# Batch 1's v by casting transfers on the software queue, and w_in one chunk of v later, in a fused attention and feed-forward kernel

## The chip, the core and the metric

The kernel runs on one core of a Trainium2 chip. The metric is the device time of one execution in microseconds (us), the median over runs. The names are those of the profile: PE (TensorE, with PEld for its weight loads), DVE (VectorE), ACT (ScalarE), POOL (GpSimd) and SP (SyncE, which here only issues transfers). POOL issues the transfers of the software queue (q0), SP those of the hardware queue (q1).

## What is computed

For 8 batches of 8 heads, 576 tokens and 64 features, two attentions are added: a local one, in which a token sees its neighbours at a distance under 4, and one over means of 4 tokens, whose result is repeated 4 times. The sum, laid out as 4608 tokens by 512 features, goes through two matrix products with a gate between them.

```python
q_d = q.reshape(B, H, Sd, factor, D).mean(axis=3)      # k_d and v_d likewise, factor 4
out_up = np.repeat(sm_attn(q_d, k_d, v_d), factor, axis=2)
mask = np.abs(pos[:, None] - pos[None, :]) < factor
out_local = np.matmul(softmax(where(mask, scores, -1e9)), v)
x = (out_up + out_local).transpose(0, 2, 1, 3).reshape(B * S, H * D)
h = x @ w_in                                            # 512 -> 2048
out = (h * sigmoid(1.702 * h)) @ w_out                  # 2048 -> 512
```

All inputs are float32 in the memory outside the core; the matrix work is in bf16.

## The kernel before

**Groups and batches.** The feed-forward part runs over `n_groups` = 9 groups of 512 tokens. Group g needs the attention of batches up to g, so the loop over g computes group g and lays batch g + 1's attention (`attention`) between its matmuls, at places counted in sixteenths (`POS_0` for g = 0, `POS` later). Batch 0's attention stands by itself ahead of the loop, and its last part is mixed with the first matmuls of group 0 (`part`, `turned`). `mm1` multiplies by w_in and ACT applies the gate (`silu`); `mm2` multiplies by w_out. In group 0, `mm2` takes w_out by quarters (`load_w_out(0)` to `load_w_out(3)`): its order of 64 matmuls needs the third quarter from matmul 32 on, and the fourth from 48.

**The order is written out.** Every engine runs its instructions in the order of the source; there is no scheduler. A dependency holds a whole engine's queue. In the built program each software-queue transfer also waits until the eighth one before it has landed, and SP's transfers do the same among themselves.

**How v comes in.** `load_v` issues ten transfers on SP, five chunks i of two halves `par`, 64 partitions by 8 heads by 64 features each, float32 into the tile `vf`. `prep_v` then casts a chunk into the bf16 tile `vbs[b % 2]` (65 columns a head: the last holds ones). For batch 0 the casts are spread: chunks 0 and 1 on ACT, 2 to 4 on DVE. For batch 1 POOL does five casts. `load_v4` fetches v in a second layout for the means; batches 0 and 1 form those means on PE instead (`prep_vd_pe`, from all five chunks of `vbs`, line 312; the result is copied out by ACT in line 321). For batch 1 that stands at `VDP_0` = 52, which is matmul 36 of `mm2`.

**Gates.** To hold a transfer back, a one-element copy writes into its target and reads what it is to wait for. Line 728 (POOL) holds `load_w_in(0, 512)` until a part of v 0's second chunk is there. `load_v(1)` is held by a DVE copy (line 708) until the first quarter of w_out has landed. Line 808 (POOL) holds `load_w_out(2)` until v 1's fourth chunk is there.

**q and k.** `load_qk` brings both by casting transfers on the software queue. `prep_qk` transposes them on DVE (line 260), and `pool_qk` adds groups of four on POOL (lines 276 and 285: four instructions for a batch's half of the heads). `scores` (line 351) and `scores_d` (line 369) are the two products on PE; ACT takes the exponentials (`exp_local`, `exp_down`). `av_local` (line 408) and `av_down` (line 430) multiply by v; `normalise` is DVE (lines 441 and 443). For batch 0, `transp_sum` (lines 483, 493, 507) turns and adds both results on PE, and `copy_x` (lines 520 and 524) copies them on ACT to `xT`.

Of the kernel before, what the change touches and what calls it, by code (L numbers as in the profile page):

```python
# [10 lines left out]
AF = mybir.ActivationFunctionType  # L11
# [8 lines left out]
def kernel(  # L20
# [9 lines left out]
    nc = tc.nc  # L30
# [41 lines left out]
    def ps_tile(n=None):  # L72
        if n is None:
            n = turn["a"] % 3
            turn["a"] += 1
        return PA[n]
# [130 lines left out]
    def load_v(b, gate=None):  # L207
# [4 lines left out]
        for i in range(5):  # L212
            for par in range(2):
# [6 lines left out]
                    ),  # L220
                )

    def load_v4(b):
        for kc in range(3):
            for j in range(2):
                nc.sync.dma_start(
                    out=v4[64 * j : 64 * j + 48, kc],
                    in_=bass.AP(
                        tensor=v.tensor,
                        offset=v[b, j].offset + kc * 48 * 4 * D,  # L230
                        ap=[[4 * D, 48], [2 * S * D, HP], [1, 4 * D]],
                    ),
                )
# [32 lines left out]
    def prep_qk(b, qd):  # L266
        prep_1("k", b, qd)
        prep_1("q", b, qd)

    def pool_qk(b, qd, names="kq"):  # L270
        for name, src in (("k", kT), ("q", qT)):
            if name not in names:
                continue
            sv = src[b, qd].rearrange("p (j f) a -> p j f a", f=4)
            t1 = work.tile([128, SD, 2, 2], FP32, name="pq", tag="pq")
            nc.gpsimd.tensor_tensor(  # L276
                out=t1, in0=sv[:, :, 0:2, :], in1=sv[:, :, 2:4, :], op=ALU.add
            )
            if name == "k":
                dst = kdT[qd][:, 0:SD, :]  # L280
            else:
                t = work.tile([128, SD, 2], BF16, name=f"qdT{qd}", tag=f"qdT{qd}", bufs=1)
                qdT[b, qd] = t
                dst = t
            nc.gpsimd.tensor_tensor(
                out=dst, in0=t1[:, :, 0, :], in1=t1[:, :, 1, :], op=ALU.add
            )
# [73 lines left out]

    def scores_d(b, qd, sd=None):
        sd = sd or ps_tile()
        for kc in range(3):
            for a in range(2):
                for r in range(4):
                    rows = slice(32 * r, 32 * r + 32)
                    j = r % 2
                    nc.tensor.matmul(  # L369
                        sd[64 * j : 64 * j + 64, r // 2, SD * kc : SD * kc + SD],  # L370
                        lhsT=kdT[qd][rows, 48 * kc : 48 * kc + 64, a],
                        rhs=qdT[b, qd][rows, :, a],
                        start=(a == 0), stop=(a == 1),
                        tile_position=(32 * r, 64 * j),
                    )
        return sd
# [8 lines left out]
    def exp_down(qd, sd):  # L385
        nc.scalar.activation(  # L386
            out=eds[qd][:, :, 0:432], in_=sd[:, :, 0:432],
            func=AF.Exp, scale=inv_sqrt_d / 16.0,
        )
# [12 lines left out]
    def av_local(b, hp, o):  # L402
        E, vb = es[hp], vbs[b % 2]
        for i in range(5):
            for par in range(2):
                for j in range(2):
                    pos = j if par == 0 else 1 - j
                    nc.tensor.matmul(  # L408
                        o[64 * pos : 64 * pos + 64, par, 65 * i : 65 * i + 65],
                        lhsT=E[64 * par : 64 * par + 64, j, 60 * i : 60 * i + 64],  # L410
                        rhs=vb[64 * par : 64 * par + 64, i, 2 * hp + j, :],
                        start=True, stop=True,
                        tile_position=(64 * par, 64 * pos),
                    )

    def av_down(b, hp, o):
        Ed, vd, u = eds[hp // 2], vds[b % 2], hp % 2

        blocks = [(kc, x, 0) for kc in range(3) for x in range(2)]
        blocks += [(0, 0, 1), (0, 1, 1), (1, 0, 1), (2, 0, 1)]  # L420
        if True:
            for kc, x, c2 in blocks:
                for j in range(2):
                    pos = j if x == 0 else 1 - j
                    c0 = 65 * (5 + c2)
                    q0 = SD * kc + 48 * (min(x + c2, 1) + x)
                    last = x == c2 == 1
                    if last:
                        q0 = 0
                    nc.tensor.matmul(  # L430
                        o[64 * pos : 64 * pos + 64, j, c0 : c0 + 65],
                        lhsT=Ed[64 * j : 64 * j + 48, u, q0 : q0 + 64],
                        rhs=vd[64 * j : 64 * j + 48, kc, hp, :],
                        start=(kc == 0), stop=(kc == 2 or last),
                        tile_position=(64 * j, 64 * pos),
                    )

    def normalise(o):
        ov = o[:, :, 0:455].rearrange("p x (c e) -> p x c e", e=65)
        rc = work.tile([128, 2, 7, 1], FP32, name="rc", tag="rc")  # L440
        nc.vector.reciprocal(rc, ov[:, :, :, 64:65])  # L441
        y = work.tile([128, 2, 7, D], BF16, name="y", tag="y", bufs=4)
        nc.vector.tensor_tensor(  # L443
            out=y, in0=ov[:, :, :, 0:D],
            in1=rc.to_broadcast([128, 2, 7, D]), op=ALU.mult,
        )
        return y
# [69 lines left out]
    def copy_x(b, hp, x):  # L517
        t0 = b * S
        for par in range(2):
            nc.scalar.copy(  # L520
                out=sub(xT[hp], t0 + 3 + 57 * par, (114, 5), (1, 57)),
                in_=sub(x[par], 3 - 3 * par, (57, 5), (1, 57)),
            )
            nc.scalar.copy(
                out=sub(xT[hp], t0 + 573 * par, (1, 3)),
                in_=sub(x[par], 285 * par, (1, 3)),
            )
# [40 lines left out]
    def warm(n):  # L568
        if n:
            t = pm_tile()  # L570
            for _ in range(n):
                nc.tensor.matmul(
                    t, lhsT=wz[:, 0:128], rhs=wz, start=True, stop=True
                )
# [132 lines left out]
    def after(src, eng):  # L707
        return lambda t: eng.tensor_copy(out=t, in_=src)
# [16 lines left out]
    sp = scores(0, 0, barred=True)  # L725
    exp_local(0, sp)
    prep_qk(0, 1)
    nc.gpsimd.tensor_copy(out=w_in_bf[0:1, 0, 0:1], in_=vf[0][0:1, 1, 0, 0:1])
    load_w_in(0, 512)
    pool_qk(0, 1)  # L730
    load_w_in(512, 512)
    load_w_in(1024, 1024)
    for qd in range(NQ):
# [16 lines left out]
        prep_v(0, nc.vector, i=slice(i, i + 1))  # L750
    warm(6)
    prep_vd_pe(0, PA[2])
    o[0] = PA[0]
    av_local(0, 0, o[0])
    av_down(0, 0, o[0])
    y[0] = normalise(o[0])
    sd = scores_d(0, 1, PA[1])
    exp_down(1, sd)
    nc.scalar.preload_act_table_set("silu_and_others")
    for hp in range(1, 3):  # L760
        o[hp] = PA[hp]
        av_local(0, hp, o[hp])
        av_down(0, hp, o[hp])
        y[hp] = normalise(o[hp])
    warm(1)

    gT0 = new_gT()
    acc = PM + [PA[n][:, u, :] for n in (1, 2, 0) for u in range(2)]
# [25 lines left out]
        silu(gT0, ffc, acc[ffc])  # L794

    def loads_2():
        load_v(2)
        load_v4(2)

    for g in range(n_groups):  # L800
        b = g + 1
        if g == 0:
            prep_qk(1, 0)
            pool_qk(1, 0)
            prep_qk(1, 1)
            load_v(1, gate=after(w_out_bf[0:1, 0, 0:1], nc.vector))
            pool_qk(1, 1)
            nc.gpsimd.tensor_copy(
                out=w_out_bf[0:1, 8, 0:1], in_=vf[1][0:1, 3, 0, 0:1]
            )  # L810
            load_w_out(2)
            load_w_out(3)
            for i in range(5):
                prep_v(1, nc.gpsimd, i=slice(i, i + 1))
            for qd in range(NQ):
                load_qk(2, qd)
            loads_2()
        elif b < B:
            if b > 2:
                load_v4(b)  # L820
            prep_qk(b, 0)
            pool_qk(b, 0)
            if b + 1 < B:
                for qd in range(NQ):
                    load_qk(b + 1, qd)
            prep_v(b, nc.gpsimd)
            if b + 1 < B:
                load_v(b + 1)
            prep_qk(b, 1)
            pool_qk(b, 1)  # L830
            prep_v4(b, nc.gpsimd)
        steps = {}
        if b < B:
            for n, f in zip(POS if g else POS_0, attention(b, None if g else (1, 2))):
                steps.setdefault(n, []).append(f)
            if g == 0:
                steps.setdefault(VDP_0, []).append(lambda: prep_vd_pe(1, PA[2]))
        gT = new_gT() if g else gT0
        mm1(g, gT, steps, 0 if g else 6)
        mm2(g, gT, {n - 16: f for n, f in steps.items() if n >= 16})  # L840
# [30 lines left out]
```

The softmax here doesn't subtract the row's maximum and nothing guards it: scores larger than these inputs give would overflow.

## Time and profile before

| what | value |
|---|---|
| median of 8 runs | 334.02 us (333.24 to 335.21) |
| the profiled execution's own time | 334.83 us |
| its span, first to last instruction | 333.0 us |
| PE busy | 318.4 us (96%), 5043 matmuls |
| ACT busy | 184.5 us (55%) |
| POOL busy | 138.2 us (42%) |
| DVE busy | 130.8 us (39%) |
| hardware queue q1 | 55056 packets, 26.95 MB, 35.3% of 16 engines' span |
| software queue q0 | 8304 packets, 13.63 MB, 23.7% |

The span is the time between the first and the last instruction of one profiled execution; that execution took 1.8 us more than its span. Busy time is summed over the whole span, so a high share says which engine is used most, not what a stretch waits for. A transfer's bytes are counted as they arrive: a cast from float32 to bf16 reads twice what is shown.

### The profile page before, as it was taken

The page shows a single profiled execution, that of the slowest core. Times are in us where ns is not written, and L with a number is a line of the kernel's source. Part 1 is how long each engine was busy: PE and PEld are TensorE (multiplying, and loading weights), DVE is VectorE, ACT ScalarE, POOL GpSimd, SP SyncE. Part 2 cuts the span into 40 slices and gives each one's busy share as a digit, 9 for nine tenths or more (in the row PEclk, how much of TensorE's full clock was granted, in tenths as well). Part 3 has the DMA queues.
Part 4 walks back from the last instruction along what each step waited for, and adds up shares of the span by engine and source line. Part 5 has one row for each costly group of instructions (what it writes and reads, how often), then busy time and mean ns, then how long its engine had stood idle before and what let it go on. Part 6 is the DMA issues. An engine that isn't in the chain of part 4 may idle for free.

```text
span 333.0 us, 11272 instructions
## 1 busy us (share of the span) xinstructions
PE 318.4 (96%) x5043; PEld 160.2 (48%) x5043; DVE 130.8 (39%) x213; ACT 184.5 (55%) x323; POOL 138.2 (42%) x168
## 2 busy tenths in 40 slices
PE   8758999999999999999999999999999999999995
PEld 3445445444554455445544454445544554444444
DVE  4837302582277216730773067406750570000000
ACT  2542487266745774566656664666466746425711
POOL 7791752019901990099109910992089000000000
PEclk9955899999999999999999999999999999999999
DMA  7999989997922993199519941993180110011011
GB/s 127 181 180 210 178 151 198 191 221 155 192 76 73 205 197 101 39 216 178 144 37 213 201 121 42 205 205 101 66 174 3 35 65 31 2 64 63 2 58 68
DMA packets 63552, 41.36 MB, mean 124 GB/s; under 512 B 44048, under 2 KB 54416, under 8 KB 63504
## 3 DMA queue, kind: packets, MB, share of 16 engines
q1 hardware_dynamic: 55056, 26.95, 35.3%
q0 software_dynamic: 8304, 13.63, 23.7%
q8 instruction: 39, 0.64, 0.8%
q14 instruction: 9, 0.07, 0.1%
q10 hardware_dynamic: 144, 0.07, 0.1%
HBM read 44.83 MB, written 9.44 MB: 163 GB/s over the span
## 4 chain that ended last, share of the span: by engine, by line
PE 89%; SPq 3%; DVE 2%; DMA 2%; issue 1%; ACT 1%; DVEq 0%; ACTq 0%
PE pm L616 36%; PE pm L672 35%; SPq L214 3%; PE pa L351 3%; PE pa L616 2%; PE pa L430 2%; PE pa L408 2%; PE pa L369 2%; DMA vf<-in_v_dram 2%; PE pa L457 2%; PE pa L672 1%; PE pm L687 1%; DVE y L443 1%; PE pa L483 1%; ACT vd L321 0%
## 5 line engine op out<-in xcount | busy, mean ns | idle before, releaser
L616 PE MATMUL pm<-xT,w_in_bf 128*128 128x512 bf16 x544 | 122.0, 381 | 0.5 <-DVE xT L559 0.5
L672 PE MATMUL pm<-w_out_bf,gT 128*128 128x512 bf16 x528 | 121.7, 380 | 0.0
L627 ACT ACTIVATE gT<-pm 128x512 bf16<-128x512 f32 x136 | 81.0, 598 | 44.5 <-PE pm L616 44.5
L616 PEld LDWEIGHTS <-w_in_bf 128*128 128x128 bf16 x576 | 55.8, 98 | 68.0 <-issue 2.0
L672 PEld LDWEIGHTS <-gT 128*128 128x128 bf16 x560 | 51.8, 98 | 59.5 <-issue 0.2
L276 POOL TENSOR_TENSOR pq<-kT 128x576 f32<-128x576 bf16 x16 | 18.5, 1159 | 106.9 <-DVE kT L260 106.9
L394 DVE TENSOR_TENSOR es<-es,mask 128x600 bf16<-128x600 bf16 x28 | 20.0, 729 | 97.1 <-ACT es L380 96.3
L657 ACT ACTIVATE osb<-pm 128x512 f32<-128x512 f32 (+2 forms) x35 | 20.8, 594 | 40.0 <-PE pm L672 36.1
L532 ACT COPY od<-pa 128x384 f32<-128x384 f32 (+1 forms) x56 | 18.4, 412 | 31.0 <-DVE y L443 18.7
L443 DVE TENSOR_TENSOR y<-pa,rc 128x896 bf16<-128x896 f32 x32 | 34.9, 1092 | 1.1
L553 DVE TENSOR_TENSOR xT<-pa,od 128x570 bf16<-128x570 f32 x28 | 21.1, 753 | 10.6 <-ACT od L532 10.5
L380 ACT ACTIVATE es<-pa 128x600 bf16<-128x600 f32 x32 | 19.8, 668 | 7.3 <-PE pa L351 7.0
L297 POOL TENSOR_TENSOR v<-v 112x512 f32<-112x512 f32 x18 | 22.8, 1265 | 0.0
L659 DVE TENSOR_SCALAR osb<-pm 128x128 f32<-128x128 f32 x1 | 0.3, 291 | 55.3 <-ACT osb L657 55.3
L260 DVE STREAM_TRANSPOSE kT<-kb 128x576 f32<-128x576 f32 x16 | 20.0, 1251 | 3.1 <-DMA kb<-in_k_dram 3.0
L260 DVE STREAM_TRANSPOSE qT<-qb 128x576 f32<-128x576 f32 x16 | 19.9, 1243 | 1.3 <-DMA qb<-in_q_dram 1.0
L276 POOL TENSOR_TENSOR pq<-qT 128x576 f32<-128x576 bf16 x16 | 18.5, 1156 | 0.0
L291 POOL CAST vb<-vf 128x2560 bf16<-128x2560 f32 (+1 forms) x11 | 17.0, 1572 | 0.0
L441 DVE RECIPROCAL rc<-pa 128x14 f32<-128x14 f32 x32 | 7.7, 241 | 23.6 <-PE pa L430 23.6
L351 PE MATMUL pa<-qT,kT 32*64 32x60 bf16 x1280 | 13.8, 203 | 2.1 <-issue 1.9
L386 ACT ACTIVATE ed<-pa 128x864 bf16<-128x864 f32 x16 | 14.3, 897 | 1.5 <-PE pa L369 1.5
L351 PEld LDWEIGHTS <-kT 32*64 32x64 bf16 x1280 | 11.9, 104 | 6.8 <-issue 5.6
(86 smaller groups left out, 254.9 us busy)
## 6 DMA issues: line engine op xcount, KB each, us to landing
vf<-in_v_dram SPq DMA_DIRECT2D x80, 128.0 KB, 5.3
out_dram<-osb SPq DMA_DIRECT2D x35, 256.0 KB, 2.0
v<-in_v_dram SPq DMA_DIRECT2D x36, 192.0 KB, 5.2
kb<-in_k_dram POOLq DMA_DIRECT2D x16, 288.0 KB, 6.7
qb<-in_q_dram POOLq DMA_DIRECT2D x16, 288.0 KB, 7.6
w_out_bf<-in_moe_w_out_dram POOLq DMA_DIRECT2D x4, 512.0 KB, 12.7
w_in_bf<-in_moe_w_in_dram POOLq DMA_DIRECT2D x2, 512.0 KB, 6.0
w_in_bf<-in_moe_w_in_dram POOLq DMA_DIRECT2D x1, 1024.0 KB, 9.9
```

The costliest lines, as they stand in the source:

```text
L260: nc.vector.transpose(out=t32.rearrange("p (i c) -> p c i", c=18), in_=store[b, qd].bitcast(FP32).rearrange("p (c d) -> p c d", c=18),)
L276: nc.gpsimd.tensor_tensor(out=t1, in0=sv[:, :, 0:2, :], in1=sv[:, :, 2:4, :], op=ALU.add)
L297: eng.tensor_tensor(out=t1[0:112], in0=x[:, :, 0:2, :], in1=x[:, :, 2:4, :], op=ALU.add)
L351: nc.tensor.matmul(sp[r // 2][64 * par : 64 * par + 64, r % 2, 60 * i : 60 * i + 60], lhsT=kT[b, qd][rows, k0 : k0 + 64, a], rhs=qT[b, qd] ...
L380: nc.scalar.activation(out=es[2 * qd + u][:, :, 0:300], in_=sp[u][:, :, 0:300], func=AF.Exp, scale=inv_sqrt_d,)
L394: nc.vector.tensor_tensor(out=ev, in0=ev, in1=mask, op=ALU.mult)
L443: nc.vector.tensor_tensor(out=y, in0=ov[:, :, :, 0:D], in1=rc.to_broadcast([128, 2, 7, D]), op=ALU.mult,)
L553: eng.tensor_tensor(out=sub(xT[hp], t0 + 3, (57, 2), (114, 5), (1, 57)), in0=sub(x, 3, (509, 2), (57, 5), (1, 57)), in1=sub(od, 3, (57, 2) ...
L616: nc.tensor.matmul(acc, lhsT=w_in_bf[:, dmc, ffc * 128 : (ffc + 1) * 128], rhs=xT[dmc][:, g * TG : g * TG + TG], start=(dmc == 0), stop=(d ...
L627: nc.scalar.activation(out=gT[:, ffc, :], in_=acc, func=AF.Silu, scale=GELU_SCALE)
L657: eng.activation(out=osb, in_=ap, func=AF.Copy, scale=1.0 / GELU_SCALE)
L672: nc.tensor.matmul(ops[t], lhsT=gT[:, ffc, t * 128 : (t + 1) * 128], rhs=w_out_bf[:, ffc, :], start=(ffc == 0), stop=(ffc == n_ffc - 1),)
```

## The change

1. The gate of `load_w_in(0, 512)` reads v 0's chunk 2 instead of chunk 1, and the k half of `pool_qk(0, 1)` moves ahead of it on POOL.
2. In batch 0's attention, the local products of heads 0 and 1 come first, then the two `av_down`; `scores_d(0, 1)` writes to the two banks `PM` instead of `PA[1]`, and its exponential becomes two instructions of 432 columns. One `warm` matmul then stands ahead of `av(0, 2, 2)`.
3. `copy_x` of the last pair of heads does its second half (`par` = 1) on DVE.
4. v 1 is no longer loaded by SP and cast by POOL. `load_vb` issues ten casting transfers on the software queue, straight into `vbs[1]`; they stand on POOL around the two `pool_qk(1, ...)`, two ahead of the first, four behind it and four behind the second, and the third and fourth quarter of w_out are issued after them. Both gates of that stage go. Both `prep_qk(1, ...)` stand ahead of them.
5. `loads_2` (v 2 and its second layout, on SP) moves from ahead of the group to place 42 of group 0, that is matmul 26 of `mm2`, and is gated on v 1's fourth chunk.

```diff
+    def load_vb(b, i):
+        for par in range(2):
+            nc.gpsimd.dma_start(
+                out=vbs[b % 2][64 * par : 64 * par + 64, i, :, 0:D],
+                in_=bass.AP(
+                    tensor=v.tensor,
+                    offset=v[b, 0].offset + (114 * i + KSTART[par]) * D,
+                    ap=[[D, 64], [S * D, H], [1, D]],
+                ),
+            )
...
     def scores_d(b, qd, sd=None):
         sd = sd or ps_tile()
+        bank = sd if sd is PM else [sd[:, u, :] for u in range(2)]
...
-                        sd[64 * j : 64 * j + 64, r // 2, SD * kc : SD * kc + SD],
+                        bank[r // 2][64 * j : 64 * j + 64, SD * kc : SD * kc + SD],
...
         for par in range(2):
-            nc.scalar.copy(
+            cp = nc.vector.tensor_copy if par and hp == HP - 1 else nc.scalar.copy
+            cp(
...
     prep_qk(0, 1)
-    nc.gpsimd.tensor_copy(out=w_in_bf[0:1, 0, 0:1], in_=vf[0][0:1, 1, 0, 0:1])
+    pool_qk(0, 1, "k")
+    nc.gpsimd.tensor_copy(out=w_in_bf[0:1, 0, 0:1], in_=vf[0][0:1, 2, 0, 0:1])
     load_w_in(0, 512)
-    pool_qk(0, 1)
+    pool_qk(0, 1, "q")
...
     prep_vd_pe(0, PA[2])
-    o[0] = PA[0]
-    av_local(0, 0, o[0])
-    av_down(0, 0, o[0])
-    y[0] = normalise(o[0])
-    sd = scores_d(0, 1, PA[1])
-    exp_down(1, sd)
-    nc.scalar.preload_act_table_set("silu_and_others")
-    for hp in range(1, 3):
+    for hp in range(2):
         o[hp] = PA[hp]
         av_local(0, hp, o[hp])
+    for hp in range(2):
         av_down(0, hp, o[hp])
         y[hp] = normalise(o[hp])
+    scores_d(0, 1, PM)
+    for u in range(2):
+        nc.scalar.activation(
+            out=eds[1][:, u, 0:432], in_=PM[u][:, 0:432],
+            func=AF.Exp, scale=inv_sqrt_d / 16.0,
+        )
+    nc.scalar.preload_act_table_set("silu_and_others")
     warm(1)
+    o[2] = av(0, 2, 2)
+    y[2] = normalise(o[2])
...
     def loads_2():
-        load_v(2)
+        load_v(2, gate=after(vbs[1][0:1, 3, 0, 0:1], nc.vector))
         load_v4(2)
...
             prep_qk(1, 0)
+            prep_qk(1, 1)
+            load_vb(1, 0)
             pool_qk(1, 0)
-            prep_qk(1, 1)
-            load_v(1, gate=after(w_out_bf[0:1, 0, 0:1], nc.vector))
+            load_vb(1, 1)
+            load_vb(1, 2)
             pool_qk(1, 1)
-            nc.gpsimd.tensor_copy(
-                out=w_out_bf[0:1, 8, 0:1], in_=vf[1][0:1, 3, 0, 0:1]
-            )
+            load_vb(1, 3)
+            load_vb(1, 4)
             load_w_out(2)
             load_w_out(3)
-            for i in range(5):
-                prep_v(1, nc.gpsimd, i=slice(i, i + 1))
             for qd in range(NQ):
                 load_qk(2, qd)
-            loads_2()
...
             if g == 0:
+                steps.setdefault(42, []).append(loads_2)
                 steps.setdefault(VDP_0, []).append(lambda: prep_vd_pe(1, PA[2]))
```

## The prediction

> **What bounds the kernel now.** First the page's slices of the span (8.3 us each): PE is full from the seventh slice on, so a change can win or lose only in the opening, or by opening a gap later.
>
> ```profile
> PE   8758999999999999999999999999999999999995
> PEclk9955899999999999999999999999999999999999
> DMA  7999989997922993199519941993180110011011
> ```
>
> PE has gaps in the first four slices, its clock is halved in slices 3 and 4, and the DMA engines are full there. Next the chain of waits, 13 to 37 us:
>
> ```profile
> 13.63 6.47 DMA vf<-in_v_dram
> 20.19 0.44 DVE vb L291
> 20.67 0.44 PE pa L312 x2
> 21.13 0.81 ACT vd L321
> ...
> 23.43 0.90 ACT ed L386
> 24.38 0.49 PE pa L408 x18
> ...
> 26.34 0.48 PE pm L483 x2
> ...
> 29.34 1.35 issue
> 30.69 0.42 PE pa L507 x12
> 31.11 0.96 PE pm L616 x2
> ...
> 36.71 0.28 PE pa L507 x20
> ```
>
> The opening waits for the last transfer of v 0 (chunk 4): issued at 13.63, landed at 20.10. The queues between 14.2 and 18.2 us say why:
>
> ```profile
> q0 software_dynamic: 515, 0.51, 89.5%
> q1 hardware_dynamic: 560, 0.14, 20.6%
> ```
>
> All 512 packets of the first w_in piece pass here, while v's queue has 20.6% of the engines. From 40.5 to 46 us, alone, v's 256-byte packets pass at 4229 in 5.5 us, 770 per us. Chunk 4 is 1024 packets; alone it would need 1.3 us. After this chain PE is busy without a gap of 0.15 us from 36.36 to 49.11 (the table by stage has 12.75 of 12.75 us).
>
> **The change, part by part.**
>
> *The gate.* POOL's timeline has the gate at 12.13 and the w_in issue at 12.60; its data begin about 14.2. Chunk 2's first half landed at 13.41, so the gate passes near 13.5 and the issue comes near 14.0, data near 15.6. In the 1.4 us gained chunk 4's 1024 packets pass at 700 to 800 per us, nearly all; they land near 16.5 (17.8 if a quarter is left behind w_in). Then DVE is next: in its timeline the casts of chunks 2 and 3 end at 18.06. Chunk 4's cast (0.43) ends at 18.5, against 20.63: **2.1 us** earlier. The k half of `pool_qk` fits into POOL's wait of 1.26 us ahead of the gate; the q half then ends near 17, earlier than the 17.78 of before. Behind it on POOL stand the other w_in pieces, so they come no later; w_in's first piece lands near 19 as before and is wanted at 28.5 at the earliest.
>
> *The order of batch 0's attention.* From PE's chunk 4 matmuls (20.67) to `transp_sum` (26.27) it is 5.6 us, with PE gaps of 0.47 (for vd) and 0.99 (for ed) in its timeline. With heads 0 and 1 together the first gap is covered by the second `av_local` (0.49). The product into `PM` ends about 3.2 us after chunk 4's matmuls; the two exponentials (0.5 each, from 0.9 for 864 columns) hold `warm` and `av_down` of pair 2 for 0.5 to 0.6. I get 5.25 us: **0.35 us** gained. `normalise` runs beside it and is ready 2 us before its reader.
>
> *`copy_x` on DVE.* ACT's four copies end at 37.87 and the matmuls that need them start at 40.39, so the path gains nothing. But batch 1's four transposes now queue on DVE behind a copy that waits for PE's last `transp_sum` (ends 36.99), where they began at 30.84. Nobody near needs them: `scores(1, 0)` is at 49.11. POOL does: see below.
>
> *v 1.* Taken away: five POOL casts (2.83 us), two gates, ten SP transfers. Added: ten POOL issues. Issues of 512 packets (w_in, w_out) took 0.75 to 0.81 us, of 128 packets (k, q) 0.56; `load_vb` has 512, so 0.78 each[...]. The data, which the trace does not show in this form: 256 bytes read, 128 written a packet. Nearest rows: plain 256-byte packets, 86.3% of 16 engines for 4229 in 5.5 us, 18 ns; casts with 1024 bytes written (20.2 to 22 us: 347 packets, 119.7%) 99 ns and 2048 bytes (23.5 to 26.8: 336, 111.0%) 174 ns. The straight line through the two casts gives 33 ns at 128 bytes. That is 32 packets an engine x 33 = 1.06 us, over the 1.15 at which cast packets overlap: 0.9 us a transfer (0.5 from the plain row). I take 0.9. [...] But this trace's four k and q transfers of 288 KB, issued 0.55 apart, landed at 30.7, 32.2, 33.6, 34.9: 1.4 us each[...]. [...]
>
> Now the chain on POOL, counted from the end of `transp_sum(3)` (T = 36.99 before): DVE's copy 0.5, first transpose 1.26, `pool_qk(1, 0)` 3.7 (32.25 to 35.94 in its timeline), four issues 3.1, `pool_qk(1, 1)` 3.7, four issues 3.1: the third quarter of w_out is issued at T + 15.4.
>
> ```profile
> DMA to landing us min/median/max: 5.9/7.5/9.2
> ```
>
> This answer for the two later quarters gives the third 5.9 us from issue to landing, of which, by its packets, 1.7 led to the first data and 2.9 was data. With v's last data ending near T + 17.5 and 2.9 + 1.0 behind them: T + 21.4. PE wants that quarter at 58.53 = T + 21.5. **Before, it landed at 51.83, T + 14.8; the change spends those 6.7 us of slack to the last 0.1.** v 1 itself is complete near T + 18.5 and wanted at T + 22.5 (59.48); the fourth quarter lands near T + 24.3, wanted at T + 28.8 (65.75); the pooled k and q are ready at T + 5.5 and T + 12.3, wanted at T + 12.8 and T + 16.5. I put **0.2 us** for the third quarter's expected lateness. The first two issues wait for w_in's last piece (28.45 before), with only `pool_qk(1, 0)` behind them, which waits longer for DVE. The four k and q issues of batch 2 move from 50.24 to about T + 17 and land by T + 30 = 67; DVE wants them at 72.33.
>
> *`loads_2` later.* Its DVE gate sits behind the masks (55.4) and finds chunk 3 there. v 2 would be complete about 69 (68.72 before) and POOL casts it at 79.48; the second layout lands by 77 (75.56), used at 85.50. SP's four stores behind it come 1 to 2 us later, and ACT has four buffers with the next store at 91.5. Nothing on the path.
>
> *The clock.* From 15.88 to 36.36 the table by stage grants PE half its clock, then all of it. The last 10.24 us of that in thirds:
>
> ```profile
> 26.12:29.53 3.41, 3.21 (x91) 2.52 (x91) 3.02 (x5) 0.83 (x4) 0.00 (x0) 0.50 1.11 211
> 29.53:32.95 3.42, 2.26 (x32) 1.18 (x35) 2.04 (x3) 0.83 (x4) 0.70 (x1) 0.50 1.11 209
> 32.95:36.36 3.41, 3.41 (x32) 1.34 (x34) 3.09 (x3) 0.83 (x4) 3.25 (x5) 0.50 1.22 205
> ```
>
> In columns: window, length, PE, PEld, DVE, ACT, POOL busy, granted clock, DMA. [...] the third stretch is the first with PE full. Of wide matmuls (line 616) the three hold 0, 1.03 and 2.74 us. If the end stood at 36.36 whatever PE does, as the row alone says, 2.45 us gained at half clock would be worth 1.2. [...] I take 2.45.
>
> **Sum.** 2.1 + 0.35 = 2.45, less 0.2: 2.25 us. On the profiled execution's own 334.83: 332.6. That execution is 0.8 above the median of 334.02, so the forecast is **331.8 us**. A measurement of this kernel can tell about 0.3%, 1.0 us.
>
> **The rivals.**
>
> *Half of it.* The half clock ends where it did: 334.02 - 1.2 = 332.8, lateness left out. For it: the trace's 36.36 is one event[...]. [...]
>
> *The gain is used up.* Either chunk 4's packets still straggle behind w_in (a quarter of them to 18 costs nothing, half of them to 19.2 costs 1.2), or the third quarter is 1.5 to 2 late: 334.02 - 2.45 + 1.75 = 333.3.
>
> *Slower: the third quarter of w_out comes late on the software queue.* It decides from 2.5 us lateness. Through the data: v's last four transfers start at T + 13.95, so break-even lies at 1.55 us a transfer, 55 to 58 ns a packet; from 1.8 us on, it is clearly slower. At 1.9 us even the middle four (data from T + 7.1) run into them: data end T + 22.3, quarter lands T + 26.2, 4.7 late: 334.02 - 2.45 + 4.7 = **336.3 us**. Through issues: eight at 1.1 instead of 0.78 do the same as 2.5. For it: 128-byte writes into rows 130 bytes apart have no row in this trace, and there is no slack. Against: both rows put the packet at 18 to 33 ns.
>
> *Not what it says.* v 1 may land no sooner than before: that is so (T + 18.5 against 47.66, T + 10.7), and it isn't what the gain rests on.
>
> **How the numbers follow.** Main case 0.45 (331.8, own range 330.8 to 332.6); half of it 0.20 (332.8, 0.13 of it faster by over 0.3%, 0.07 within); used up 0.15 (333.3, of which 0.02 faster); slower 0.20. Faster, under 333.0: 0.45 + 0.13 + 0.02 = 0.60; same 0.07 + 0.13 = 0.20; slower 0.20. The range runs from 330.6 ([...]PE's last gaps may close a little too; 0.05 lies below) to 335.8, some way into the slower case, so that 0.14 lies above.
>
> **What would show it.** Right: the last v 0 transfer lands near 16.5 to 17.8, PE's chunk 4 matmuls come near 18.5, `transp_sum(0)` near 23.8, and line 672's 33rd matmul waits under 0.5 us. Wrong: a PE gap at matmul 32 of group 0's `mm2`, released by w_out's transfer, above 2.5 us; `load_vb` landings more than 1.5 us apart; chunk 4 still landing past 19; a second stretch of half clock. After group 0 both traces should agree but for the shift.

## The result and the profile after

| | before | changed |
|---|---|---|
| median | 334.42 us (32 runs) | 330.7 us (11 runs, 329.12 to 332.8) |
| the profiled execution's own time | 334.83 us | 331.78 us |
| its span | 333.0 us | 330.0 us |

The ratio is 0.9887 with a 95% interval of 0.9865 to 0.9908. The changed kernel is 3.8 us faster, between 3.1 and 4.5. The forecast was 2.25 us faster, 331.8 us, in a range from 330.6 to 335.8.

The slices of the page of the changed kernel (8.25 us each) answer to the three lines shown of before:

```profile
PE   8777999989999999999999999999999999999996
PEclk9985999999999999999999999999999999999999
DMA  7999989999913993299329931994180110011012
```

The third slice of PEclk has risen from 5 to 8, and of the opening only the fourth is still at half clock. PE has gaps in the first four slices in both kernels; behind them its digits are 9, but for the last slice and one 8 in the ninth slice of the changed kernel. So the gain lies in the opening. Where exactly is shown by PE's timeline of the changed kernel. Its columns are start, length of the group, engine, line, operation, and in brackets the idle time ahead of the group with what ended it.

```profile
14.73 2.04 PE L585 MATMUL pm<-wz 128*128 128x512 bf16 x6
16.70 1.71 PE L323 MATMUL pa<-vb,psel 128*64 128x256 bf16 x14
18.34 0.73 PE L420 MATMUL pa<-vb,es 64*64 64x65 bf16 x40
19.30 0.57 PE L442 MATMUL pa<-vd,ed 48*64 48x65 bf16 x40 [0.23 <-ACT vd L332]
19.80 0.58 PE L381 MATMUL pm<-qdT,kdT 32*64 32x144 bf16 x24
20.99 0.38 PE L585 MATMUL pm<-wz 128*128 128x512 bf16 x1 [0.62 <-ACT ed L775]
...
21.77 0.37 PE L495 MATMUL pm<-up,y 128*64 128x285 bf16 x4
...
23.46 0.25 PE L519 MATMUL pa<-ident,y 60*64 60x60 bf16 x6
27.01 0.42 PE L519 MATMUL pa<-ident,y 60*64 60x57 bf16 x14 [3.31 <-issue]
27.36 1.03 PE L629 MATMUL pm<-xT,w_in_bf 128*128 128x512 bf16 x2
```

The wait for v 0's chunk 4 is gone: the last row of `prep_vd_pe` (line 323) runs through, and its last matmul ends at 18.41. `transp_sum(0)` (line 495) begins at 21.77. Then comes a gap of 3.31 us that the profile puts down to "issue": PE waited for nothing that the trace shows as data. The same lines of the kernel before, for the two ends of that wait, are these.

```profile
20.67 0.43 PE L312 MATMUL pa<-vb,psel 128*64 128x256 bf16 x2 [1.91 <-DVE vb L291]
...
26.27 0.55 PE L483 MATMUL pm<-up,y 128*64 128x285 bf16 x4
...
30.69 0.42 PE L507 MATMUL pa<-ident,y 60*64 60x57 bf16 x14 [1.35 <-issue]
31.04 1.03 PE L616 MATMUL pm<-xT,w_in_bf 128*128 128x512 bf16 x2
```

From these rows the lead of the changed kernel, stretch by stretch:

| PE reaches | before | changed | lead gained in the stretch |
|---|---|---|---|
| end of the matmuls on chunk 4 | 21.11 | 18.41 | +2.70 |
| `transp_sum(0)` | 26.27 | 21.77 | +1.80 |
| first wide matmul of group 0 | 31.04 | 27.36 | -0.82 |
| `scores(1, 0)` | 49.11 | 45.37 | +0.06 |
| end of the span | 333.0 | 330.0 | -0.74 |

The lead at `transp_sum(0)` is 4.5 us. The issue wait takes back 1.96 of it (3.31 against 1.35), and the rest of that stretch is 1.14 shorter. Of the end's -0.74 no more is read than this: the timeline of the changed kernel has another issue wait of 0.74 at 66.75, that of before has none between 60 and 90 us.

The table by stage tells what the clock did. Columns: window, its length, busy time and instructions of PE, PEld, DVE, ACT and POOL, granted clock, DMA share, GB/s. First before, then the changed kernel.

```profile
12.46:15.88 3.42, 1.56 (x75) 0.89 (x52) 3.35 (x7) 1.84 (x4) 3.18 (x4) 1.00 1.07 136
15.88:36.36 20.48, 15.60 (x312) 9.36 (x312) 12.89 (x16) 6.89 (x17) 13.54 (x16) 0.50 1.11 197
```

```profile
12.07:15.48 3.41, 1.82 (x88) 1.13 (x85) 3.27 (x11) 2.33 (x5) 2.13 (x5) 1.00 0.85 147
15.48:18.90 3.42, 3.42 (x58) 1.88 (x57) 2.36 (x4) 1.99 (x4) 3.34 (x5) 0.50 1.09 160
18.90:25.73 6.83, 3.96 (x211) 3.12 (x203) 5.07 (x8) 3.42 (x8) 6.79 (x8) 1.00 1.17 199
25.73:32.55 6.82, 5.54 (x58) 2.39 (x59) 0.00 (x0) 1.66 (x8) 0.82 (x2) 0.50 1.11 211
```

Half clock lasted 20.48 us before and 10.24 us after, in two pieces, and the stretch from 18.90 to 25.73, where the heads of batch 0 run, was at full clock. The second row of the lead table, 1.80, is the sum of two things: the new order shortens that stretch by 0.7 us when both kernels are at half clock (the order alone, below), and by difference 1.1 us goes with the full clock. Full clock came back at 18.90, behind a window in which PE was busy throughout, since the wait for chunk 4 is gone. Before, PE's gap of 1.91 us ahead of 20.67 lies inside the half clock.

The traces point to a fetch of PE's own instructions as the cause of the issue wait. The queues of the changed kernel inside the gap, from 24.5 to 25.6 us (queue, packets, MB, share of 16 engines):

```profile
q0 software_dynamic: 105, 0.22, 104.1%
q8 instruction: 1, 0.02, 5.3%
```

One packet of 16 KB on queue 8, begun at 24.60, lasts 0.94 us, and PE goes on at 27.01. The packet of before began at 28.43. From 23.5 to 24.5 us, inside the gap, q8 has none, and the software queue has a share of 117.4%: the fetch had not begun while w_in filled the engines. In all thirteen traces of this case PE stops at the same matmul, or reaches it without a gap that shows, and starts it 2.2 to 2.4 us after that packet begins.

The longer wait of the changed kernel is not a longer fetch. From the matmul that stands 128 ahead to the matmul behind the wait it took 5.73 us before (24.96 to 30.69) and 5.70 us in the changed kernel (21.31 to 27.01). PE started all 128 matmuls within 4.1 us at half clock and within 2.2 us at full clock, and then waited for the same moment, 5.7 us after the first. So what the full clock gained in that stretch was lost again in the wait.

### The profile page after: what moved, and what is told of

Read it like the earlier page. It is cut to its first block, busy times and chain, and to the rows that moved or that the text cites. A ratio compares the mean times of both kernels' runs of the same rounds, so it can differ in the third digit from the quotient of the medians.

```text
span 330.0 us, 11262 instructions
## 1 busy us (share of the span) xinstructions
PE 315.6 (96%) x5043; PEld 158.3 (48%) x5043; DVE 129.8 (39%) x215; ACT 184.1 (56%) x322; POOL 142.0 (43%) x172
## 4 chain that ended last, share of the span: by engine, by line
PE 91%; issue 3%; DVE 1%; DMA 1%; POOL 1%; ACT 1%; POOLq 0%; ACTq 0%; DVEq 0%
PE pm L629 36%; PE pm L685 35%; PE pa L362 4%; PE pa L629 2%; PE pa L442 2%; PE pa L381 2%; PE pa L420 2%; PE pa L469 2%; PE pa L685 2%; DMA kb<-in_k_dram 1%; PE pm L700 1%; PE pa L323 1%; PE pm L585 1%; POOL pq L287 1%; PE pa L495 1%
## 5 line engine op out<-in xcount | busy, mean ns | idle before, releaser
L566 DVE TENSOR_TENSOR xT<-pa,od 128x570 bf16<-128x570 f32 x28 | 21.1, 753 | 11.3 <-ACT od L545 11.2
L311 POOL TENSOR_TENSOR vd<-v 112x256 bf16<-112x256 f32 x18 | 13.7, 759 | 1.4
L302 POOL CAST vb<-vf 128x2560 bf16<-128x2560 f32 x6 | 14.2, 2362 | 0.0
```

Source lines behind the costliest of these rows:

```text
L566: eng.tensor_tensor(out=sub(xT[hp], t0 + 3, (57, 2), (114, 5), (1, 57)), in0=sub(x, 3, (509, 2), (57, 5), (1, 57)), in1=sub(od, 3, (57, 2) ...
```

## Experiments

The question after the result: the forecast had the gate at 2.1, the order at 0.35, v 1 at nothing. Which term was wrong, and what does the issue wait depend on?

### The gate alone

To the kernel before, only this:

```diff
-    nc.gpsimd.tensor_copy(out=w_in_bf[0:1, 0, 0:1], in_=vf[0][0:1, 1, 0, 0:1])
+    pool_qk(0, 1, "k")
+    nc.gpsimd.tensor_copy(out=w_in_bf[0:1, 0, 0:1], in_=vf[0][0:1, 2, 0, 0:1])
     load_w_in(0, 512)
-    pool_qk(0, 1)
+    pool_qk(0, 1, "q")
```

> The kernel before with the new gate alone (w_in waits for v 0's chunk 2, the k half of pool_qk ahead of it). Theory A, the gate is the gain: chunk 4 of v 0 lands near 16.5 us instead of 20.1, PE's chunk 4 matmuls end near 18.4 instead of 21.1, PE has no gap of 1.9 us at 20.67 any more, the clock comes back near 19 us, and the time falls by 2.4 to 3.6 us. Rival B, the new order of batch 0's attention carries half of it: 1.5 to 2 us.

Measured: 331.87 us against 334.11, ratio 0.9932 (0.9912 to 0.9951), 2.3 us faster (1.6 to 2.9). Chunk 4 landed at 16.18 and 16.65. The issue wait is still there: PE's timeline of this kernel has

```profile
23.04 0.55 PE L483 MATMUL pm<-up,y 128*64 128x285 bf16 x4 [0.47 <-issue]
27.62 0.31 PE L507 MATMUL pa<-ident,y 60*64 60x57 bf16 x14 [1.64 <-issue]
```

The term of 2.1 us for the gate holds. The 2.3 us lie between the two forecasts of this run, and the interval reaches into both, so it doesn't refute the rival that gives the order half of the gain. The clock came back later than forecast: half clock lay from 22.19 to 25.60 and from 29.01 to 32.43.

### The order alone

To the kernel before, only part 2 of the change (`scores_d` into `PM`, the local products of heads 0 and 1 first, one `warm` ahead of `av(0, 2, 2)`).

```diff
-    o[0] = PA[0]
-    av_local(0, 0, o[0])
...
-    for hp in range(1, 3):
+    for hp in range(2):
         o[hp] = PA[hp]
         av_local(0, hp, o[hp])
+    for hp in range(2):
         av_down(0, hp, o[hp])
```

> The kernel before with the new order of batch 0's attention alone (both av_local first, scores_d(0, 1) into PM). Theory A: chunk 4 still lands at 20.1, the gaps of 0.47 and 0.99 us go, one of about 0.6 comes; at most 0.5 us faster, the same by measurement, because PE then waits again near the 350th to 480th matmul (in both traces 5.7 us lie between these two, with a wait that the profile gives to issue: 1.35 us before, 3.31 after). Rival B: 1.5 us or more faster.

Measured: 331.91 us against 334.11, ratio 0.9938 (0.9913 to 0.9963), 2.1 us faster (1.2 to 2.9). The prediction had 0.35, which the interval excludes, and rival B came true. PE's timeline of this kernel shows the fetch wait nearly gone:

```profile
25.08 0.55 PE L484 MATMUL pm<-up,y 128*64 128x285 bf16 x4
...
28.33 0.42 PE L508 MATMUL pa<-ident,y 60*64 60x57 bf16 x14 [0.18 <-issue]
28.69 1.03 PE L617 MATMUL pm<-xT,w_in_bf 128*128 128x512 bf16 x2
```

The first local product starts at 20.52; from there to `transp_sum(0)` it is 4.56 us, before it was 5.25 (21.02 to 26.27): 0.7 us. From `transp_sum(0)` to the first wide matmul it is 3.61, before 4.77: 1.16, and the issue wait is 1.17 of that (0.18 for 1.35).

One execution could be a coincidence, so a second execution of both was profiled, on one chip.

> The kernel before once more, for a second profile. If the begin of the instruction fetch is set by the order of transfers alone, it comes 3.5 us after the second local product of pair 2 again; if it depends on chance in the queues, it moves by more than 1 us. [...]

> The kernel of e2_order once more, for a second profile. If the new order by itself shortens the fetch wait (0.18 us in its first profile, against 1.35 before), it is under 0.5 again; if that was chance, it is 1 to 3 us.

Measured: 334.44 us (before) and 333.75 us (order alone), one execution each. The timelines, before first:

```profile
21.19 0.43 PE L312 MATMUL pa<-vb,psel 128*64 128x256 bf16 x2 [2.37 <-DVE vb L291]
...
31.14 0.42 PE L507 MATMUL pa<-ident,y 60*64 60x57 bf16 x14 [1.28 <-issue]
```

```profile
22.26 0.43 PE L312 MATMUL pa<-vb,psel 128*64 128x256 bf16 x2 [3.35 <-DVE vb L291]
...
30.94 0.42 PE L508 MATMUL pa<-ident,y 60*64 60x57 bf16 x14 [0.69 <-issue]
```

In this pair the order's kernel began the matmuls on chunk 4 1.07 us later and was still 0.2 us ahead at the matmul behind the fetch: 1.27 us caught up, 0.59 of it in the fetch wait. The wait of 0.69 lies between the two forecasts (under 0.5, and 1 to 3). So the two parts, 0.7 from the shorter stretch and 0.6 to 1.2 from the fetch wait, show in both pairs of traces. They make 1.3 to 1.9 of the 2.1 us; the remainder is inside the interval, and a part of it may be the clock (below).

### v 1 and its neighbours alone

To the kernel before, parts 3 to 5 (`load_vb`, `loads_2` at place 42, `copy_x` on DVE), with the old gate and order:

```diff
             prep_qk(1, 0)
-            pool_qk(1, 0)
             prep_qk(1, 1)
-            load_v(1, gate=after(w_out_bf[0:1, 0, 0:1], nc.vector))
+            load_vb(1, 0)
+            pool_qk(1, 0)
+            load_vb(1, 1)
+            load_vb(1, 2)
             pool_qk(1, 1)
...
-                prep_v(1, nc.gpsimd, i=slice(i, i + 1))
...
-            loads_2()
```

> The kernel before with the rest of the change (v 1 by casting transfers on the software queue, loads_2 later, the last half of copy_x on DVE), with the old gate and the old order. Theory A: the same, within 0.4 us; w_out's third quarter lands within 0.5 us of the matmul that wants it. Rival C, the software queue takes load off and group 0 runs with fewer waits: 1 us or more faster. Rival D, that quarter comes late: up to 1 us slower, with a PE gap at matmul 32 of group 0's second product.

Measured: 334.62 us against 334.11, ratio 1.0006 (0.9978 to 1.0034): no difference, as theory A had it. The third quarter of w_out is late by this much, in the timeline:

```profile
57.30 1.02 PE L685 MATMUL pm<-w_out_bf,gT 128*128 128x512 bf16 x4 [0.34 <-DMA w_out_bf<-in_moe_w_out_dram]
```

### All but the gate

To the changed kernel:

```diff
-    pool_qk(0, 1, "k")
-    nc.gpsimd.tensor_copy(out=w_in_bf[0:1, 0, 0:1], in_=vf[0][0:1, 2, 0, 0:1])
+    nc.gpsimd.tensor_copy(out=w_in_bf[0:1, 0, 0:1], in_=vf[0][0:1, 1, 0, 0:1])
     load_w_in(0, 512)
-    pool_qk(0, 1, "q")
+    pool_qk(0, 1)
```

> The changed kernel with the old gate (w_in waits for chunk 1, pool_qk behind it). Theory A: nearly all of the gain goes, 0 to 0.8 us faster than before. Rival B: 1.5 to 2.5 us faster remains.

Measured: 332.04 us against 334.11, ratio 0.9948 (0.9923 to 0.9972), 1.7 us faster: theory A was wrong, and rival B came true. With the order at 2.1 and v 1 at about -0.2, that closes: the order's gain does not need the gate. The ratios of gate alone and order alone multiply to 0.987, and the whole change has 0.9887. In this kernel's timeline PE has no wait for its instructions of 0.15 us or more:

```profile
25.54 0.55 PE L495 MATMUL pm<-up,y 128*64 128x285 bf16 x4
...
28.21 0.64 PE L519 MATMUL pa<-ident,y 60*64 60x60 bf16 x20
28.79 0.61 PE L629 MATMUL pm<-xT,w_in_bf 128*128 128x512 bf16 x2
```

### Is the issue wait a fetch held up by the transfers?

If it is, it must shrink when less stands on the software queue at the time. In this run, the quiet kernel, the last 1 MB of w_in of the changed kernel, and all that POOL issues behind it, are held until the first of the two exponentials into `eds[1]`:

```diff
     load_w_in(512, 512)
-    load_w_in(1024, 1024)
-    for qd in range(NQ):
-        load_qk(1, qd)
-    load_w_out(0)
-    load_w_out(1)
-    nc.gpsimd.memset(v4[32:64], 0.0)
...
     nc.scalar.preload_act_table_set("silu_and_others")
+    nc.gpsimd.tensor_copy(out=w_in_bf[0:1, 0, 1024:1025], in_=eds[1][0:1, 0, 0:1])
+    load_w_in(1024, 1024)
+    for qd in range(NQ):
+        load_qk(1, qd)
+    load_w_out(0)
+    load_w_out(1)
+    nc.gpsimd.memset(v4[32:64], 0.0)
```

> The changed kernel with w_in's last piece (1 MB) and all that follows it on the software queue held, by a copy on POOL, until the exponential of scores_d(0, 1) is there (21.4 us), so that the DMA engines are idle for a stretch near 22.5 to 24 us. Theory F: the wait of 3.31 us in the middle of transp_sum for pair 1, given to issue, is PE's instructions coming late behind the transfers (a fetch of 16 KB on the queue for instructions began at 24.60 and PE went on at 27.01; before, 28.43 and 30.69). With the engines idle the fetch begins near 22.6, the wait falls under 1.6 us, and the time falls by 1 to 2 us below the changed kernel's; all landings behind move by 3 us, which none of their readers feels before w_out's third quarter. Rival G: the wait belongs to PE's own pace at this place and not to the transfers: it stays near 3 us, and the time is the same or up to 1 us slower by the later landings.

Measured: 330.89 us against 333.78, ratio 0.9924 (0.9899 to 0.9949). Two rows of PE's timeline tell both halves of the story:

```profile
24.77 0.31 PE L519 MATMUL pa<-ident,y 60*64 60x57 bf16 x14 [1.10 <-issue]
...
53.48 1.87 PE L685 MATMUL pm<-w_out_bf,gT 128*128 128x512 bf16 x4 [3.20 <-DMA w_out_bf<-in_moe_w_out_dram]
```

The fetch began at 22.37 (24.60 in the changed kernel), the issue wait is 1.10 instead of 3.31, and `transp_sum(0)` stands where it stood (21.73). The wait is 1.96 and 3.31 in the two profiles of the changed kernel, and 2.36 and 3.01 in two runs below whose edits stand behind this place; with the hold it is 1.10 here and 0.54 in the last run. From the matmul 128 ahead to the packet's begin, the DMA share is 0.97 and 0.92 in the two runs with the hold, and 1.11 to 1.18 in the other eleven traces. So with the order and the gate of the changed kernel the wait did shrink with the load of the transfers. The forecast of the time failed: it was to fall 1 to 2 us below the changed kernel's, and the ratio is 0.0037 higher. The same hold makes w_out's third quarter late by 3.20 us, which theory F had not priced.

### Is w_out's third quarter really without slack?

To the changed kernel (this run is the delayed kernel), one POOL memset, of a tile that holds the same zeros already, ahead of the issue:

```diff
             load_vb(1, 4)
+            nc.gpsimd.memset(v4[32:64], 0.0)
             load_w_out(2)
```

> The changed kernel with one more memset of 2.65 us on POOL ahead of the third quarter of w_out. Theory E, all the slack of that quarter is spent (landed at 54.78, wanted at 54.8): PE gets a gap of 2.3 to 2.9 us at matmul 32 of group 0's second product and the time grows by as much, 333 to 334. Rival, there is slack left that the trace does not show: the same time as the changed kernel.

Measured: 333.6 us against 333.78, ratio 0.9991 (0.9964 to 1.0018). The memset takes 2.65 us and turns into this wait:

```profile
56.99 1.02 PE L685 MATMUL pm<-w_out_bf,gT 128*128 128x512 bf16 x4 [2.29 <-DMA w_out_bf<-in_moe_w_out_dram]
```

What is left of the changed kernel's gain of 3.8 us lies between 1.2 us faster and 0.6 us slower than before. The ratio rose by 0.0104, about 3.5 us with an uncertainty of 1.2: the wait of 2.29 is the larger part of it, and the rest is at the edge of the error. The slack at that place is at most 0.4 us (2.65 less 2.29).

### `copy_x` on ACT again, and the changed kernel again

```diff
-            cp = nc.vector.tensor_copy if par and hp == HP - 1 else nc.scalar.copy
+            cp = nc.scalar.copy
```

> The changed kernel with all of copy_x on ACT again. By the prediction's step, copy_x on DVE gains nothing and only delays batch 1's transposes and POOL behind them: the same time within 0.4 us, with the transposes starting near 30 us instead of 34.2 and w_out's third quarter landing 2 to 3 us ahead of its reader. Rival, the DVE half shortens the path to the first gated matmuls: 0.5 us or more slower without it.

> The changed kernel once more, for a second profile. Theory F: the wait in transp_sum for pair 1 follows the begin of the instruction fetch by 2.2 to 2.5 us again, wherever that begin falls; the stretches of half clock may lie elsewhere. [...]

Measured: with ACT's copies 329.38 us against 333.78, ratio 0.9875 (0.9848 to 0.9901), not to be told from the whole change's 0.9887. The transposes began at 29.96, as forecast. The third quarter was issued at 44.20 (48.45 in the changed kernel), landed at 52.09 and was wanted at 53.29: 1.2 us ahead, where 2 to 3 were forecast, since it took 7.9 us from issue to landing instead of 6.3. So the DVE copy spends about a microsecond of that quarter's slack and gains nothing.

The changed kernel itself, in one more execution, took 329.76 us, with half clock for 3.41 us only and an issue wait of 1.96. The packet began at 24.40 and PE went on at 26.59, 2.19 later, as theory F had it:

```profile
27.84:31.25 3.41, 3.41 (x36) 1.31 (x33) 0.00 (x0) 0.83 (x4) 0.68 (x1) 0.50 1.13 215
```

The two profiled executions of the changed kernel thus differ by 6.83 us of half clock. In this one the third quarter landed at 53.50, wanted at 53.54.

### Both waits taken away

The hold of the quiet kernel, with `copy_x` on ACT, and the third quarter issued right behind v 1's first chunk:

```diff
             load_vb(1, 0)
+            load_w_out(2)
             pool_qk(1, 0)
...
             load_vb(1, 4)
-            load_w_out(2)
             load_w_out(3)
```

> The kernel of f1_quiet with w_out's third quarter issued behind v 1's first chunk instead of behind the last, and copy_x on ACT as in f4_act. Theory F with E: the wait in transp_sum for pair 1 stays near 1.1 us, the third quarter lands near 44 and v 1 near 49, both ahead of their readers (near 50 and 51), the gap of 3.2 us of f1_quiet is gone; 1.5 to 2.5 us faster than the changed kernel, 327.5 to 329 where before is 334. Rival: v 1's last chunk or the fourth quarter becomes late instead, and the time stays at 329.5 to 331.

Measured: **327.79 us** (326.47 to 329.08) against 333.96, ratio 0.9811 (0.9762 to 0.986), 6.3 us faster than before (4.7 to 7.9) and as forecast. The changed kernel's ratio is 0.9887, and its interval (0.9865 to 0.9908) doesn't touch this one; the 0.0076 between them are 2.5 us. Against the changed kernel with ACT's copies (0.9875) the difference is 0.0064, 2.1 us, and these two intervals overlap a little. What the shorter wait is worth apart from the earlier third quarter is not shown. The timeline of this run and its table by stage:

```profile
24.73 0.31 PE L519 MATMUL pa<-ident,y 60*64 60x57 bf16 x14 [0.54 <-issue]
...
50.09 1.03 PE L685 MATMUL pm<-w_out_bf,gT 128*128 128x512 bf16 x4
```

```profile
15.80:26.00 10.20, 7.30 (x279) 5.02 (x277) 7.76 (x13) 5.92 (x14) 6.31 (x11) 1.00 0.98 145
26.00:36.40 10.40, 10.29 (x99) 5.07 (x96) 3.43 (x3) 6.77 (x18) 7.37 (x8) 1.00 1.12 208
```

No stretch of half clock is left in this opening, the issue wait is 0.54, and `mm2`'s 33rd matmul waits for nothing: the third quarter landed at 46.10.

## Why the prediction was right, and which of its terms were not

**The direction and the place were right; the size was luck in part.** The gain comes from the opening, and behind it the lead is nearly kept (3.74 us at `scores(1, 0)`, 3.0 at the end). But the forecast gives nearly all of it to chunk 4, and by themselves the gate is worth 2.3 us and the order 2.1. The median, 330.7, lies only 0.1 us inside the range, and the main case's 2.25 us lies outside the interval of 3.1 to 4.5: the gain was forecast at 0.6 of its size. One reading is wrong without consequence: PE's digits are 9 from the fifth slice on, not the seventh.

**The gate: right.** The forecast had chunk 4's matmuls near 18.5, and their group has no wait and ends at 18.41. The expected 2.1 us is 2.70 in this trace and 2.3 (1.6 to 2.9) by itself. In the second profiles chunk 4 landed at 20.61 before and at 18.43 changed, later than the 17.8 that the prediction allowed, and its matmuls ended at 21.62 and 19.34: 2.28 us. So the step's size holds, with a landing that moves by almost 2 us between traces with the new gate (16.65 in the gate alone, 18.43 here). Where the chunk is early, DVE's casts are next. The working took DVE's casts of chunks 2 and 3 to end at 18.06 as before, and chunk 4's at 18.5. In DVE's timeline of before and of the changed kernel:

```profile
13.16 1.81 DVE L182 TENSOR_SCALAR psel<-dp,rv 128x64 bf16<-128x64 f32 x2
```

```profile
13.62 0.58 DVE L182 TENSOR_SCALAR psel<-dp,rv 128x64 bf16<-128x64 f32 x2
16.28 1.56 DVE L302 CAST vb<-vf 128x512 bf16<-128x512 f32 x3
```

The pair that makes `psel` took 1.81 us beside `pool_qk`'s k half on POOL, and 0.58 us now that this half is done ahead of the gate. In the thirteen traces the pair takes 0.58 in the eight where no tensor operation of POOL runs beside it, and 1.35 to 2.16 in the five where one does. All three casts end at 17.84 here. With the gate alone they end at 18.44, as forecast: there the step that makes `du` takes 1.96 us beside `pool_qk`'s q half (0.76 before).

**The order: the term that failed.** The prediction put it at 0.35 us, from 5.6 to 5.25 between the matmuls on chunk 4 and `transp_sum`. By itself the order is worth 2.1 us (1.2 to 2.9). The stretch itself gained 0.7: the gaps that the prediction names, 0.47 and 0.99, are 0.20 and 0.61 in the first trace of the order alone. The sum put the fetch of PE's instructions behind it at nothing: that wait is 1.35 and 1.28 us in the two traces of before, 0.18 and 0.69 with the new order, and under 0.15 in the changed kernel without its gate. The row stood in the chain of waits that the prediction showed (`29.34 1.35 issue`) and was given no cause.

**The fetch wait in the changed kernel was not foreseen.** It grew from 1.35 to 3.31 us and took back 1.96 of the 4.5 us lead at `transp_sum(0)`; the forecast of 23.8 for that matmul was 2.0 too late. At the first wide matmul 2.45 us gained would have been 28.6 (31.04 less 2.45); it came at 27.36, so the wait cancels a part of the other error. That instructions come in pieces of 16 KB on a queue of their own is on the page (39 packets, 0.64 MB, on queue 8). In the changed kernel their cost moved with the transfers: the wait was 3.31 us with the software queue at 117.4% and 104.1% of the engines in two stretches inside it, and 1.10 with the last MB of w_in held back.

**The clock: less of it at half, in whole steps.** The sum took half clock to end 2.45 us sooner, because work is earlier by that much; that was the author's estimate. What happened is that half clock covered 20.48 and 13.65 us in the two profiles of before, and 10.24 and 3.41 us in the two of the changed kernel. These are six, four, three and one times 3.41.

What stood ahead of half clock can be read off the traces. With the time of the twelve traces that have half clock cut into windows of 3.41 us, at the edges of the stretches, all fifteen windows at full clock that half clock followed have PE busy for 0.4 to 1.87 us, as the windows 12.46 to 15.88 (1.56) and 12.07 to 15.48 (1.82) above. All 1080 at full clock that full clock followed have 1.80 us or more. Full clock came back behind windows with 2.95 us or more, and stayed away behind those with up to 3.24. The longest gap ahead of half clock in the first trace of before is 1.86 us, 13.05 to 14.91. The prediction named "a second stretch of half clock" as a sign of error: there is one in the changed kernel, 25.73 to 32.55, behind a window with PE busy for 1.4 us because of the fetch wait. No run tested by itself what starts half clock.

How much of the gain goes with the clock can be estimated from the runs. The mean granted clock of each run gives 14.4 us of half clock on average before (62 runs; 12.4 and 14.6 in two smaller sets), 9.8 with the gate alone, 11.3 with the order alone and about 6 in the changed kernel (11 runs). Among the 62 runs of before, 1 us more of half clock goes with 0.2 us more time. By that, an estimate, the clock carries 1.3 to 1.7 of the 3.8 us, 0.9 of the gate's 2.3 and 0.6 of the order's 2.1.

**v 1 on the software queue: right, on the edge.** Expected 0.2 us of lateness for the third quarter. Alone it is late by 0.34 us, with no measurable time (1.0006). In the changed kernel it landed at 54.78 and the matmul that needs it began at 54.82: T + 21.5 and T + 21.6 with T = 33.25, where T + 21.4 and T + 21.5 were forecast. v 1's issues were a little cheaper than the 0.78 us taken, in POOL's timeline:

```profile
39.32 2.74 POOL L225 DMA_DIRECT2D vb<-in_v_dram  x4
```

Four take 2.74 us, 0.70 each by the median of 703 ns. Transfers of v 1 that were issued one behind the other landed 0.3 to 1.0 us apart (42.51, 43.51, 44.17 and 44.77 for the first group of four), so the 0.9 us a transfer that the forecast took from its rows was near: 0.75 on average in that group.

**The rivals.** *Half of it* (1.2 us gained) and *used up* (0.7) lie outside the interval of 3.1 to 4.5. *Slower by the third quarter* (336.3) was refuted in its price, not in its place: v 1's transfers land at most a microsecond apart, not 1.9. With 2.65 us of delay put in by hand most or all of the gain is gone: that place decides, as the rival had it. `copy_x` was costed at nothing, and nothing is what it showed. `loads_2` was costed at nothing too; it was run only together with v 1, where the sum is nothing within 0.9 us.

**What stays open.** Why the fetch begins sooner with the new order. PE waits at the 7th of 20 matmuls of `transp_sum`'s last group for pair 1, 128 matmuls behind the third of `av_local(0, 2, ...)` in the changed kernel. (The 39 packets of queue 8 for 5043 matmuls are one for every 129.) From the matmul 128 ahead the packet begins

- 3.35 to 3.5 us later in the four traces with the old order (before twice, the gate alone, v 1 alone),
- 1.5, 1.7 and 2.2 with the new order and the old gate,
- 2.2 and 3.3 in the changed kernel, 2.3 with ACT's copies and 3.0 in the delayed kernel,
- 1.1 and 0.5 in the two runs with the hold.

The last line goes with the lighter load on the DMA engines. The load does not explain the difference between before and the order alone: between 22 and 26 us the table by stage has a DMA share of 1.12 and 1.15 for them. Nor is it known why the changed kernel has 2.2 in one execution and 3.3 in another.

## What to carry to other kernels

A gap that the profile puts down to "issue" ahead of a matmul is a cost that can have a cause: before the sum is made, look for the instruction queue's packet in it, and for what fills the DMA engines at that moment. Work that reaches such a place sooner may only wait longer there, as it did here, 3.31 us for 1.35. Slack in a transfer is a number worth working out to a tenth, as here, where 2.65 us of delay used most or all of the gain. When half clock is part of the opening, price a change over many runs: here two profiles of one kernel differed by 6.83 us of half clock.

## What was not expected of the hardware

- PE waited up to 3.31 us where one 16 KB packet of the instruction queue came in, which itself lasted 0.94 us. It went on 2.2 to 2.4 us after the packet began, in all thirteen traces.
- Half clock came in whole multiples of 3.41 us in the openings, and the same kernel had six and four of them, or three and one, in two executions. In twelve traces it began behind windows with PE busy for at most 1.87 of 3.41 us.
- DVE's two `psel` instructions took 1.35 to 2.16 us beside a POOL tensor operation and 0.58 us without it.
